# GpSimd's operations placed beside VectorE's clamps, V in three parts, a shorter head and another table, in a one-core mix of full and local attention

## The chip, the cores and the metric

The kernel runs on one core of a Trainium2 chip. The core has five engines that each work through their own list of instructions and wait for one another through semaphores: TensorE (PE in the profile; its weight loads are the row PEld), VectorE (DVE), ScalarE (ACT), GpSimd (POOL) and SyncE (SP), which here only issues DMA transfers. The metric is the time of one execution on the device in microseconds. Three timed runs of the kernel before gave 810.4, 808.63 and 810.71 us, a median of 810.4.

## What is computed

For one sequence of 2048 tokens with 640 features and 32 heads of 20 features, two attentions over the same x are mixed by a gate per token:

```python
x = A_x                                             # 1 x 2048 x 640, bf16
g = sigmoid((x * gate_w).sum(-1, keepdims=True))
a = A_ref(x, A_wqkv, A_wo)   # full softmax attention, every key for every query
b = B_ref(x, B_wqkv, B_wo)   # 8 keys per query: the token and 7 earlier ones, 2 apart
return g * a + (1 - g) * b
```

Branch A is most of the work: 32 heads x 2048 queries x 2048 keys of scores, exponentials and weighted sums.

## The kernel before

**Tiling of branch A.** Four heads form a quad q (8 quads), 512 queries a chunk qc (4 chunks). A pair (qc, q) is a group; there are 32, in the order of the list `GROUPS`: first the quads 0 to 3 of query chunks 0 and 1 in turn, then quads 4 to 7 of these chunks, then chunks 2 and 3. A group goes over 16 blocks of 128 keys and 4 heads, so it has 64 units, each a block of 128 keys x 512 queries of one head; 2048 units in all. `qk` (L1654) makes two or three units' scores in PSUM, `exp` (L1678) turns them into weights on ScalarE into `ebuf`, and `pv` (L1723) multiplies them by V (`vA`, with a column of ones that gives the sum) and adds into the bank `obank`, where a whole group is gathered.

**Units ridden on VectorE.** Some units don't go to ScalarE. They are taken in quads of up to four units (all heads of one key block, called d). VectorE clamps a unit's scores out of PSUM and rounds them to 16-bit integers whose bits are read as a bf16 weight (`uD`, L1668, called the clamp). To even out the error, three more copies of the whole quad, shifted by a constant, are made from `uD` (`eD`, L902, the shifted copies, in `gen_d`), and each is multiplied on PE by its own weighted copy of V. These weighted copies are `vS`: GpSimd multiplies the quad's V block by three constants (L894, also in `gen_d`, ahead of the shifted copies). `wanted` decides when a quad is opened and a unit ridden: two buffers of `uD` must allow it, and thresholds on VectorE's idle time and on how long the group still lasts.

**Closing a group.** `close` starts `gen_norm`: VectorE transposes `obank` to `oTt` (L863) and takes reciprocals of the sums (L867); GpSimd multiplies these by the gate (L869, 16 numbers per partition) and the 512 columns of `oTt` by the result (L875, called the norm product); VectorE transposes back (L877) and SP writes the pieces to `oTd` for the output projection. The last group does the products on VectorE.

**Side work.** Generators hand out small pieces of other work between the scores: `gen_v` projects V in two halves of 320 columns (quads 0 to 3, then 4 to 7), each over the 16 key blocks, with a cast by VectorE (L831); the first half starts with the loop, the second with group 1. `gen_kd` projects K in five chunks of features (VectorE L678 and L681, then DMAs into `kT`); chunk f may start at the group `KWAIT[f]`. `gen_qd` makes the scaled queries and their bounds, `gen_gate` the gate. `gen_bproj` and `gen_b` are branch B in eight units of 256 tokens (products on VectorE at L974 and L1073, sums on PE); they need V complete, because they reuse the memory of its weights. `gen_fold` projects both branches to the output.

**Order.** The order of every engine's list is written by a planner when the program is built. It goes through the 709 score tiles in turn, keeps an assumed time for each engine, and gives out side work as long as it fits before the next scores are due. Each task is given an assumed length and the buffers that it reads and writes; from these come the semaphore waits. Tasks marked `port`, and all of GpSimd's, are assumed not to run at the same time, since both engines then need the same way to SBUF. The table `PLAN` gives, from tile number on, 18 settings: slack before scores, when quads open, how far ahead VectorE may be booked, priorities.

**Head.** x comes in four blocks of 512 tokens. Nine warm-up matmuls run until the first block has landed; PE transposes each block (`turn`, L1369) into PSUM, ScalarE and VectorE copy it out (`x_out`), and PE projects K for quad 0 (L1392). After the first `turn` four more warm-up matmuls follow (L534). GpSimd pads the first K weights (L603) and fills `kT` for quads 1 to 7 with ones (L1441). `v_first` projects the first V block (320 columns).

Of the kernel before, what the change touches and what calls it, by code (L numbers as in the profile page):

```python
# [37 lines left out]
KWAIT = (0, 0, 3, 5, 7)  # L38
# [14 lines left out]
    0: ((0.3, 0.64), 0.31, 1.0, 2.5, 0.49, -0.95, -0.1, 11.8, 7.0, 6.03, 0.52, 0.85, 4.4, 4.0, 0.0, 0.64, 3, -1.5),  # L53
    5: ((0.29, 0.69), 0.16, 1.0, 6.6, 1.12, -1.6, 0.17, 11.8, 7.0, 7.54, 0.6, 0.62, 4.85, 4.42, 0.0, 0.65, 2, -3),
    10: ((0.29, 0.69), 0.01, 1.0, 6.6, 1.12, -1.6, 0.17, 11.8, 2.0, 7.54, 0.6, 0.62, 4.85, 4.42, 0.0, 0.65, 2, -3),
    15: ((0.3, 0.63), 0.39, 1.0, 5.5, 0.79, -1.37, -1.15, 7.47, 2.0, 6.29, 0.6, 0.62, 5.69, 3.17, -0.08, 0.63, 2, -3),
    30: ((0.34, 0.51), 0.25, 1.0, 5.5, 0.87, -1.26, -0.43, 13.15, 7.0, 4.65, 0.7, 0.51, 5.31, 4.81, 0.08, 0.39, 1, -3),
    35: ((0.34, 0.51), 0.25, 1.0, 5.5, 0.87, -1.6, -0.43, 9.86, 7.0, 4.65, 0.7, 0.43, 5.31, 3.66, 0.2, 0.61, 1, -3),
    40: ((0.34, 0.58), 0.25, 1.0, 5.5, 0.87, -1.6, -0.43, 8.24, 7.0, 4.65, 0.7, 0.43, 5.31, 3.66, 0.2, 0.61, 1, -3),
    45: ((0.34, 0.58), 0.25, 1.0, 5.5, 0.87, -1.6, -0.43, 8.24, 7.0, 5.73, 0.7, 0.43, 5.31, 3.66, 0.2, 0.61, 1, -3),  # L60
    65: ((0.34, 0.58), 0.25, 1.0, 5.5, 0.87, -1.6, -0.43, 8.24, 7.0, 5.73, 0.69, 0.43, 4.7, 4.27, 0.2, 0.61, 1, -3),
    80: ((0.34, 0.58), 0.25, 1.0, 5.5, 0.87, -1.6, -0.43, 8.24, 7.0, 5.73, 0.69, 0.36, 4.7, 4.27, 0.2, 0.61, 1, -3),
    85: ((0.2, 0.8), 0.39, 1.0, 1.0, 0.81, -0.84, -0.81, 6.61, 7.0, 8.75, 0.01, 0.61, 5.68, 4.3, 0.0, 0.71, 2, -3),
    100: ((0.2, 0.8), 0.39, 1.0, 1.0, 0.81, -0.84, -0.81, 4.77, 7.0, 8.75, 0.01, 0.61, 5.68, 4.3, 0.0, 0.71, 2, -3),
    105: ((0.2, 0.8), 0.39, 1.0, 1.0, 0.81, -0.84, -0.81, 4.77, 7.0, 8.75, 0.01, 0.61, 5.68, 3.61, 0.0, 0.86, 2, -6),
    115: ((0.2, 0.8), 0.39, 1.0, 1.0, 0.81, -0.84, -0.81, 4.77, 7.0, 8.75, 0.01, 0.61, 5.68, 3.61, 0.2, 0.86, 2, -6),
    120: ((0.2, 0.8), 0.39, 1.0, 1.0, 0.63, -0.84, -1.89, 4.77, 7.0, 8.75, 0.01, 0.61, 5.68, 3.61, 0.2, 0.86, 2, -6),
    125: ((0.2, 0.73), 0.39, 1.0, 1.0, 0.63, -0.84, -1.89, 4.77, 7.0, 8.75, 0.01, 0.61, 5.68, 3.61, 0.2, 0.86, 2, -6),
    130: ((0.22, 0.73), 0.39, 1.0, 1.0, 0.63, -0.84, -1.89, 4.77, 6.7, 8.75, 0.01, 0.61, 5.68, 3.61, 0.2, 0.86, 2, -6),
    135: ((0.22, 0.73), 0.39, 1.0, 1.0, 0.77, -0.84, -1.89, 4.77, 6.7, 8.75, 0.01, 0.61, 5.63, 3.61, 0.2, 0.86, 2, -6),  # L70
    145: ((0.19, 0.73), 0.39, 1.0, 1.0, 0.77, -0.84, -1.89, 4.77, 6.7, 8.75, 0.01, 0.61, 5.63, 3.61, 0.2, 0.98, 2, -6),
    150: ((0.34, 0.68), 0.01, 2.5, 1.0, 1.25, -1.06, 0.05, 7.4, 7.0, 10.69, 0.6, 0.55, 3.3, 5.42, 0.0, 0.61, 1, -1.5),
    155: ((0.26, 0.75), 0.39, 1.0, 1.0, 0.81, -1.29, -0.97, 6.5, 7.0, 7.16, 0.43, 0.75, 4.4, 4.0, 0.0, 0.71, 0, 0),
    160: ((0.31, 0.76), 0.33, 2.5, 1.0, 0.82, -1.6, -0.34, 11.8, 6.2, 6.64, 0.82, 0.44, 4.4, 4.12, 0.0, 0.55, 2, 0),
    165: ((0.31, 0.76), 0.33, 2.5, 1.0, 0.82, -1.6, -0.34, 10.41, 7.0, 6.64, 0.34, 0.44, 3.87, 4.12, 0.0, 0.66, 2, 0),
    170: ((0.31, 0.76), 0.33, 2.5, 1.0, 0.82, -1.17, -0.34, 10.41, 7.0, 6.64, 0.34, 0.44, 3.87, 4.12, 0.0, 0.7, 2, 0),
    175: ((0.3, 0.63), 0.07, 5.5, 6.3, 0.94, -1.06, 0.05, 7.4, 2.0, 8.96, 0.6, 0.67, 3.3, 5.42, -0.14, 0.53, 1, -1.5),
    180: ((0.3, 0.63), 0.07, 5.5, 6.3, 0.69, -1.06, 0.05, 7.95, 2.0, 8.96, 0.6, 0.67, 3.3, 5.42, -0.14, 0.53, 1, -1.5),
    185: ((0.3, 0.69), 0.19, 5.5, 6.3, 0.69, -1.06, 0.05, 7.95, 2.0, 8.96, 0.6, 0.6, 3.3, 5.42, -0.14, 0.53, 1, -1.5),
    205: ((0.3, 0.66), 0.25, 2.5, 1.0, 0.94, -1.6, 0.49, 9.86, 2.0, 5.3, 0.57, 0.43, 5.64, 3.66, 0.0, 0.61, 0, 0),  # L80
    210: ((0.29, 0.69), 0.16, 1.0, 2.5, 0.94, -1.37, 0.17, 9.99, 7.0, 7.54, 0.6, 0.62, 5.69, 5.04, 0.0, 0.54, 2, -3),
    215: ((0.31, 0.72), 0.39, 1.0, 1.0, 0.94, -1.6, -0.5, 9.86, 5.5, 6.93, 0.52, 0.73, 4.64, 4.42, 0.0, 0.67, 2, -3),
    225: ((0.23, 0.7), 0.25, 2.5, 2.5, 0.83, -1.37, 0.49, 7.4, 5.5, 6.11, 0.6, 0.67, 7.13, 5.42, 0.0, 0.61, 1, 0),
    230: ((0.3, 0.63), 0.25, 1.0, 2.5, 0.83, -1.37, 0.49, 7.4, 5.5, 6.11, 0.43, 0.67, 7.13, 5.42, -0.2, 0.61, 1, 0),
    235: ((0.3, 0.63), 0.25, 1.0, 2.5, 0.83, -1.37, 0.49, 7.4, 5.5, 6.11, 0.43, 0.67, 7.78, 5.42, 0.0, 0.61, 1, 0),
    240: ((0.29, 0.69), 0.16, 1.0, 1.0, 0.94, -1.37, 0.17, 9.99, 7.0, 7.54, 0.6, 0.62, 5.69, 5.04, 0.0, 0.54, 2, -3),
    245: ((0.29, 0.69), 0.07, 1.0, 6.3, 0.94, -1.06, 0.05, 9.99, 2.0, 7.54, 0.6, 0.67, 4.79, 5.04, 0.0, 0.54, 2, -3),
    250: ((0.29, 0.58), 0.39, 6.6, 2.5, 0.94, -1.26, -0.43, 7.15, 7.0, 6.93, 0.67, 0.73, 5.56, 4.42, 0.0, 0.67, 1, -3),
    260: ((0.3, 0.53), 0.39, 1.0, 2.5, 0.94, -1.26, -0.43, 7.4, 7.0, 8.84, 0.67, 0.73, 4.45, 4.42, 0.0, 0.67, 1, -3),
    265: ((0.3, 0.53), 0.39, 5.5, 2.5, 0.94, -1.26, -0.43, 7.4, 7.0, 8.84, 0.67, 0.69, 4.45, 4.42, 0.0, 0.67, 1, -3),  # L90
    270: ((0.29, 0.69), 0.07, 2.5, 2.5, 1.39, -1.2, 0.05, 5.48, 2.0, 8.84, 0.54, 0.55, 5.43, 4.07, 0.0, 0.69, 2, -3),
    280: ((0.29, 0.69), 0.07, 2.5, 2.5, 1.39, -1.2, 0.05, 5.48, 2.0, 8.84, 0.54, 0.54, 5.43, 4.07, 0.0, 0.46, 2, -3),
    290: ((0.29, 0.69), 0.07, 2.5, 2.5, 1.39, -1.49, 0.05, 9.99, 7.0, 8.84, 0.6, 0.54, 5.31, 5.04, 0.08, 0.46, 2, -3),
    295: ((0.29, 0.69), 0.24, 2.5, 1.0, 0.94, -0.86, -0.5, 7.4, 7.0, 7.54, 0.67, 0.45, 4.4, 4.81, 0.0, 0.77, 2, -3),
    305: ((0.23, 0.63), 0.25, 2.5, 2.5, 0.94, -1.29, 0.49, 7.4, 5.5, 6.11, 0.43, 0.43, 5.56, 3.83, 0.0, 0.61, 1, 0),
    315: ((0.3, 0.63), 0.16, 1.0, 2.5, 0.94, -1.46, 0.26, 6.5, 5.5, 7.16, 0.43, 0.75, 6.57, 4.3, -0.1, 0.43, 1, 0),
    320: ((0.3, 0.66), 0.25, 2.5, 2.5, 0.73, -1.17, 0.49, 7.4, 2.0, 5.3, 0.63, 0.52, 5.64, 3.24, 0.0, 0.61, 1, 0),
# [96 lines left out]
class _Sched:  # L194
# [7 lines left out]
    def __init__(self, nc, ctx):  # L202
# [10 lines left out]
        self.mode = None  # L213
        self.busy = []
        self.port = {"dve": [], "pool": []}
        self.dma_final = {}

    def ready(self, *keys, to="pe"):
        t = 0.0
# [1696 lines left out]
```

## Time and profile before

| | |
|---|---|
| timed runs | 810.4, 808.63, 810.71 us, median 810.4 |
| the profiled execution's own time | 809.44 us |
| its span, first to last instruction | 807.5 us |
| ScalarE busy | 779.4 us (97%) |
| TensorE busy | 751.3 us (93%) |
| VectorE busy | 721.5 us (89%) |
| GpSimd busy | 124.9 us (15%) |
| exponential tiles on ScalarE | 709, of 1024 or 1536 columns |
| clamps / shifted copies on VectorE | 380 / 285 |
| vS / norm products on GpSimd | 95 / 31 |

In a group of instructions the row has the line, the engine, the operation, output and input with their shapes, the count, then the busy time in us and the mean length of one in ns, then the idle time of the engine just ahead of them and what ended most of it. Neighbouring instructions of an engine overlap a little, so the busy time of a group is less than count times mean. In a row of a timeline stand start and length in us; in square brackets the idle time before it and what it waited for. In a row by stretch, each engine has its busy time and, in brackets, its instructions.

### The profile page before, as it was taken

The numbers are of one execution on the slowest core, as the hardware profiler recorded it, in microseconds if no ns is written. First come the engines' busy times: TensorE is split into PE (matmuls) and PEld (weight loads), VectorE is DVE, ScalarE is ACT, GpSimd is POOL, SyncE is SP. The second block draws the span as 40 slices with busy tenths as digits, with TensorE's granted clock in tenths as the row PEclk, the third lists the DMA queues.
The fourth block names the chain that finished last, engine by engine and source line by source line (L and its number), as shares of the span: only waits on it lengthen the run. The fifth ranks groups of instructions, "written<-read, shape, count | busy, mean of one in ns | idle before, by whom it ended". The sixth has DMA issues, their size and how long they took to land.

```text
span 807.5 us, 28461 instructions
## 1 busy us (share of the span) xinstructions
PE 751.3 (93%) x12073; PEld 284.8 (35%) x12073; DVE 721.5 (89%) x1243; ACT 779.4 (97%) x741; POOL 124.9 (15%) x196
## 2 busy tenths in 40 slices
PE   8999999999998898999999998999999899999987
PEld 5432322232333343233334333343333433334232
DVE  7686999999889999899988999998998899899892
ACT  4999999999999999999999999999999999999996
POOL 6010111111110221120111110101120111211110
PEclk9999999999999999999999999999999999999999
DMA  9111111011301131300013122013002210300121
GB/s 308 47 28 41 30 23 40 15 28 23 85 15 31 32 75 26 79 16 24 21 22 81 31 55 45 12 24 95 13 14 53 66 20 15 77 28 7 39 65 37
DMA packets 61154, 36.08 MB, mean 45 GB/s; under 512 B 26661, under 2 KB 59829, under 8 KB 61029
## 3 DMA queue, kind: packets, MB, share of 16 engines
q1 hardware_dynamic: 60740, 33.94, 17.2%
q8 instruction: 96, 1.57, 0.8%
q10 hardware_dynamic: 288, 0.33, 0.1%
q14 instruction: 30, 0.24, 0.1%
HBM read 12.85 MB, written 3.54 MB: 20 GB/s over the span
## 4 chain that ended last, share of the span: by engine, by line
DVE 29%; PE 27%; ACT 27%; issue 13%; SPq 1%; DMA 1%; POOL 0%; DVEq 0%; ACTq 0%
ACT ebuf L1678 27%; DVE uD L1668 11%; PE score L1654 8%; DVE eD L902 8%; PE obank L1723 7%; PE side L637 6%; DVE kvw L1073 3%; PE score L637 2%; DVE qkvB L948 2%; SPq L956 1%; DVE kvw L974 1%; DVE oB L1106 1%; PE score L1369 1%; DVE oTt L863 1%; PE obank L534 1%
## 5 line engine op out<-in xcount | busy, mean ns | idle before, releaser
L1678 ACT ACTIVATE ebuf<-score 128x1024 bf16<-128x1024 f32 (+1 forms) x709 | 767.7, 1225 | 11.7 <-PE score L1654 9.2
L1654 PE MATMUL score<-qT,kT 32*128 32x512 bf16 x1856 | 257.5, 384 | 30.6 <-ACT ebuf L1678 18.1
L1668 DVE TENSOR_SCALAR uD<-score 128x512 int16<-128x512 f32 x380 | 250.2, 678 | 19.3 <-PE score L1654 18.5
L902 DVE TENSOR_SCALAR eD<-uD 128x2048 int16<-128x2048 int16 x285 | 197.3, 717 | 2.6 <-PE obank L1723 1.5
L1723 PE MATMUL obank<-ebuf,vA 128*21 128x512 bf16 x1668 | 156.0, 385 | 4.4 <-DVE eD L902 1.6
L1654 PEld LDWEIGHTS score<-qT,kT 32*128 32x128 bf16 x1856 | 64.3, 91 | 231.4 <-ACT ebuf L1678 150.2
L894 POOL TENSOR_TENSOR vS<-vA,vw 128x252 bf16<-128x252 bf16 x95 | 68.2, 721 | 344.8 <-PE obank L1723 299.9
L1723 PE MATMUL obank<-eD,vS 128*21 128x512 bf16 x1140 | 99.3, 379 | 0.0
L637 PE MATMUL side<-xT,wBs 128*32 128x256 bf16 x2300 | 92.3, 281 | 2.0 <-DVE qkvB L948 1.6
L637 PEld LDWEIGHTS side<-xT,wBs 128*32 128x32 bf16 x2300 | 65.6, 142 | 30.2 <-issue 14.9
L1723 PEld LDWEIGHTS obank<-ebuf,vA 128*21 128x21 bf16 x1668 | 37.0, 89 | 88.2 <-issue 58.6
L869 POOL TENSOR_TENSOR rcp<-rcp,gA 128x16 f32<-128x16 f32 x31 | 7.2, 233 | 298.5 <-DVE rcp L867 289.6
L1073 DVE TENSOR_TENSOR kvw<-kvw,eB 128x2048 bf16<-128x2048 bf16 x40 | 49.0, 1242 | 1.3 <-DMA kvw<-qkvB 1.3
L974 DVE TENSOR_TENSOR kvw<-qkvB 128x2048 bf16<-128x2048 bf16 x40 | 49.0, 1243 | 0.0
L948 DVE CAST qkvB<-side 128x512 bf16<-128x512 f32 (+1 forms) x69 | 40.0, 590 | 0.9 <-PE side L637 0.5
L1723 PE MATMUL obank<-uD,vA 128*21 128x512 bf16 x380 | 37.1, 379 | 0.0
L1723 PEld LDWEIGHTS obank<-eD,vS 128*21 128x21 bf16 x1140 | 28.0, 92 | 18.1 <-issue 1.4
L875 POOL TENSOR_TENSOR oN<-oTt,rcp 128x512 bf16<-128x512 f32 x31 | 32.7, 1053 | 2.4
L863 DVE STREAM_TRANSPOSE oTt<-obank 128x512 f32<-128x512 f32 x32 | 22.6, 707 | 10.2 <-PE obank L1723 10.1
L637 PE MATMUL side<-xT,kvw 128*32 128x512 bf16 (+1 forms) x360 | 29.4, 382 | 1.4 <-DVE qkvB L678 1.3
L1654 PE MATMUL score<-woBp,kT 32*128 32x512 bf16 x192 | 27.9, 384 | 0.9 <-ACT ebuf L1678 0.6
L637 PE MATMUL side<-xT,WqP 128*32 128x512 bf16 x340 | 25.7, 382 | 0.1
(191 smaller groups left out, 548.8 us busy)
## 6 DMA issues: line engine op xcount, KB each, us to landing
kvw<-qkvB SPq DMA_DIRECT2D x128, 80.6 KB
wBs<-in_B_wqkv_dram SPq DMA_DIRECT2D x1, 2400.0 KB
WqP<-in_A_wqkv_dram SPq DMA_DIRECT2D x14, 160.0 KB
oTd<-oN SPq DMA_DIRECT2D x108, 20.0 KB
out_dram<-outsb SPq DMA_DIRECT2D x12, 160.0 KB
qT<-dst SPq DMA_DIRECT2D x93, 20.0 KB
kvw<-in_A_wqkv_dram SPq DMA_DIRECT2D x2, 800.0 KB
oTd<-in_A_x_dram SPq DMA_DIRECT2D x2, 640.0 KB
```

Source lines behind the costliest of these rows:

```text
L637: ins = e.matmul(o[j:k, :], l(j) if callable(l) else l[:, j:k], r, start=(first and i == 0), stop=(last and i == n - 1), skip_group_check= ...
L863: T("dve", 0.625, lambda e: e.transpose(oTt[:, :], obank[:, :]), reads=["obank"], writes=["oTt"])
L875: T(en, c2, lambda e: e.tensor_tensor(oo, ii, ib, ALU.mult), reads=["rcp", "oTt"], writes=["oN0"])
L894: T("pool", 0.607, lambda e: e.tensor_tensor(vS[:, d % 2, :, :], _ap(vA, (kb * NQ + q) * 4 * DV, [[0, K - 1], [1, 4 * DV]]), _ap(vw, 0, [[ ...
L902: T("dve", 0.065 + 0.1334 * n, lambda e, k=k, sl=sl: e.tensor_scalar(eD[:, sl % NS, 0:512 * n].bitcast(I16), uD[d % 2][:, 0:512 * n].bitca ...
L948: t = TB(dvc(n * TOK), lambda e, o=o, i=i: e.tensor_copy(o, i), reads=[("side", b)], writes=[key])
L974: TB(dvc(CH, 2), lambda e: e.tensor_tensor(o, i0, i1, ALU.mult), reads=["qB", "kB"], writes=[("prod", i)] + (["WkA", "WvA", ("WkP", 0)] if ...
L1073: TB(dvc(CH, 2), lambda e: e.tensor_tensor(o, i0, i1, ALU.mult), reads=["eB"] + [("vR", w4) for w4 in range(4)], writes=[("prod", i)], por ...
L1654: ins = e.matmul(o, kT[32 * j:32 * j + 32, q, kb * P:(kb + 1) * P], qT[qbuf[g]][32 * j:32 * j + 32, :], start=True, stop=True)
L1668: t = T("dve", 0.598, lambda e: e.tensor_scalar(uD[d % 2][:, 512 * i:512 * (i + 1)].bitcast(I16), side[x], UOFF, 0.0, op0=ALU.add, op1=ALU ...
L1678: exps[s] = T("act", actc(512 * n), lambda e: e.activation(ebuf[s % NE][:, 0:512 * n], score[s % 2][:, 0:512 * n], ACTF.Exp, scale=LN2 / S ...
L1723: ins = e.matmul(obank[32 * j:32 * j + DV, :], v, src, start=(kb == 0), stop=(last and k >= len(lst) - 4), skip_group_check=True)
```

## The change

There are five parts. First, the planner remembers the last VectorE task marked `port` (`last_port`), and a task can be told to wait for further tasks (`after`). Second, `vS` leaves `gen_d` for a generator of its own, `gen_vs`, added when a quad is opened; it, the small gate product and the norm product, which is now two halves of 256 columns, each wait in the planner for a "slot": right after a clamp has been written into VectorE's list the first waiting generator may go on, or after 4.0 us (vS) or 3.0 us (norm). The task then waits on the chip for the last `port` task of VectorE. The shifted copies wait in the planner until `vS` has been issued. Third, V is projected in three parts: quads 0 and 1, 2 and 3 (160 columns each), 4 to 7 (320 columns), started with the loop, with group 1 and with group 3. Fourth, in the head the four warm-up matmuls after the first transposes go, the fills of `kT` for quads 5 to 7 move into `gen_kd`, K's second chunk waits for group 2, and some assumed lengths are others. Fifth, `PLAN` has other rows (110 instead of 106).

```diff
-KWAIT = (0, 0, 3, 5, 7)
+KWAIT = (0, 2, 3, 5, 7)
 PLAN = {
-    0: ((0.3, 0.64), 0.31, 1.0, 2.5, 0.49, -0.95, -0.1, 11.8, 7.0, 6.03, 0.52, 0.85, 4.4, 4.0, 0.0, 0.64, 3, -1.5),
-    5: ((0.29, 0.69), 0.16, 1.0, 6.6, 1.12, -1.6, 0.17, 11.8, 7.0, 7.54, 0.6, 0.62, 4.85, 4.42, 0.0, 0.65, 2, -3),
...
+    0: ((0.3, 0.63), 0.16, 1.0, 1.0, 0.94, -1.37, -0.29, 4.03, 5.5, 8.32, 0.45, 0.75, 5.69, 5.04, -0.2, 0.54, 1, -3),
+    10: ((0.3, 0.63), 0.16, 1.0, 1.0, 0.94, -1.37, -0.29, 4.03, 6.2, 8.32, 0.45, 1.01, 5.69, 5.04, -0.2, 0.54, 1, -3),
...
+        for a in after:
+            add(a, True)
...
+        if port and stream == "dve":
+            self.last_port = t
...
+            for q in {1: (5,), 2: (6, 7)}.get(f, ()):
+                kt_fill(q)
...
-    def gen_v(half):
-        for kb in range(NV0 if half == 0 else 0, KBN):
+    VPART = ((0, 2), (2, 4), (4, NQ))
+    vpart = lambda q: 0 if q < 2 else 1 if q < 4 else 2
+
+    def gen_v(part):
+        q0, q1 = VPART[part]
+        c0, n = 4 * DH * q0, 4 * DH * (q1 - q0)
+        for kb in range(NV0 if part == 0 else 0, KBN):
...
+        if en == "pool":
+            yield ("slot", sch.avail["pe"] + SLOTW[1])
         T(en, c1, lambda e: e.tensor_tensor(rcp[:, :], rcp[:, :], gA[qc % 2][:, :], ALU.mult),
-          reads=["rcp", ("gA", qc % 2)], writes=["rcp"])
+          reads=["rcp", ("gA", qc % 2)], writes=["rcp"], after=last_port() if en == "pool" else ())
...
+        for i, n in ((0, 4),) if en == "dve" else ((0, 2), (2, 2)):
...
+            if en == "pool":
+                yield ("slot", sch.avail["pe"] + SLOTW[1])
+            T(en, c2 if n == 4 else 0.56, lambda e, oo=oo, ii=ii, ib=ib: e.tensor_tensor(oo, ii, ib, ALU.mult), reads=["rcp", "oTt"],
+              **{"accum" if i else "writes": ["oN0"]}, after=last_port() if en == "pool" else ())
...
-        while cur["pv"] < d - 1 or not done.get(("v", kb, q // 4)) or not done.get("vw"):
+        while not done.get(("vs", d)):
             yield ("cond",)
-        T("pool", 0.607, lambda e: e.tensor_tensor(
...
+    last_port = lambda: [sch.last_port] if sch.last_port else []
+
+    def gen_vs(d):
+
+        g, kb = dquads[d]
+        q = GROUPS[g][1]
+        while cur["pv"] < d - 1 or not done.get(("v", kb, vpart(q))) or not done.get("vw"):
+            yield ("cond",)
+        yield ("slot", sch.avail["pe"] + SLOTW[0])
+        if closed[d] and not ridden[d]:
+            return
+        T("pool", 0.607, lambda e: e.tensor_tensor(
+            vS[:, d % 2, :, :], _ap(vA, (kb * NQ + q) * 4 * DV, [[0, K - 1], [1, 4 * DV]]), _ap(vw, 0, [[1, K - 1], [0, 4 * DV]]), ALU.mult),
+          reads=[("vA", kb, vpart(q)), "vAones", "vw"], writes=[("vS", d % 2)], after=last_port())
+        done[("vs", d)] = True
...
+        elif req[0] == "slot":
+            if not force and now < req[1]:
+                return False
...
+    SLOTW = (4.0, 3.0)
+
+    def slot():
+
+        for ent in sorted(gens, key=lambda e: e[0]):
+            if ent[3][0] == "slot":
+                step(ent, 0.0, True)
+                return
...
     turn(0)
-    for i in range(4):
-        T("pe", 0.215, warm_up, reads=[("qabs", 0)], writes=["obank"])
     x_out(0)
...
+        if q < 5:
+            kt_fill(q)
...
+            add_gen(gen_vs(len(dquads) - 1), 1.0)
...
             bank_free[x] = t.end + LAT["dve"]
+            slot()
...
                 if g1 == 1:
                     add_gen(gen_gate(0), 1.5)
+                    add_gen(gen_v(1), 2.9)
+                if g1 == 2:
                     add_gen(gen_gate(1), 1.6)
-                    add_gen(gen_v(1), 3)
+                if g1 == 3:
+                    add_gen(gen_v(2), 3)
```

## The prediction

> **What bounds the kernel now.** I read the page's busy times first, then the groups of instructions by line, then the chain of the first 24 us, then VectorE's and GpSimd's timelines side by side, and last the busy times by stretch.
>
> The page and its costliest groups:
>
> ```profile
> PE 751.3 (93%) x12073; PEld 284.8 (35%) x12073; DVE 721.5 (89%) x1243; ACT 779.4 (97%) x741; POOL 124.9 (15%) x196
> ...
> L1678 ACT ACTIVATE ebuf<-score 128x1024 bf16<-128x1024 f32 (+1 forms) x709 | 767.7, 1225 | 11.7 <-PE score L1654 9.2
> ...
> L1668 DVE TENSOR_SCALAR uD<-score 128x512 int16<-128x512 f32 x380 | 250.2, 678 | 19.3 <-PE score L1654 18.5
> L902 DVE TENSOR_SCALAR eD<-uD 128x2048 int16<-128x2048 int16 x285 | 197.3, 717 | 2.6 <-PE obank L1723 1.5
> ```
>
> ScalarE's exponentials fill 767.7 of 807.5 us and wait 11.7 us. The first begins at 19.60 and the last ends at 799.5, so the span is a head of 19.6, a full ScalarE, and a tail of 8 us. Of the 2048 score units (one 128x512 block of one head), 1668 go to ScalarE and 380 are ridden on VectorE (a clamp, then three shifted copies per quad of four). The time can fall in two ways only: a shorter head or tail, or more units on VectorE.
>
> The head, from the chain that ended last, cut to its first 24 us (start, length, what):
>
> ```profile
> 5.24 1.88 PE score L1369 x20
> 7.12 0.86 PE obank L534 x4
> 7.99 1.12 PE score L1369 x20
> ```
>
> The four warm-up matmuls stand on the chain between the first and second transposed block of x.
>
> GpSimd against VectorE, two answers of the timeline, VectorE's lines first (start, length, what):
>
> ```profile
> 359.24 0.23 DVE L867 RECIPROCAL rcp<-oTt 128x16 f32<-128x16 f32 x1
> 359.40 0.62 DVE L1668 TENSOR_SCALAR uD<-score 128x512 int16<-128x512 f32 x1
> 359.94 1.51 DVE L902 TENSOR_SCALAR eD<-uD 128x2048 int16<-128x2048 int16 x1
> ```
>
> ```profile
> 359.55 0.22 POOL L869 TENSOR_TENSOR rcp<-rcp,gA 128x16 f32<-128x16 f32 x1 [7.85 <-DVE rcp L867]
> 359.85 1.06 POOL L875 TENSOR_TENSOR oN<-oTt,rcp 128x512 bf16<-128x512 f32 x1
> 360.85 1.06 POOL L894 TENSOR_TENSOR vS<-vA,vw 128x252 bf16<-128x252 bf16 x1
> ```
>
> A shifted copy (median 0.683 us) that meets the norm product takes 1.51, ending 0.55 after the product does; then vS (median 0.609) takes 1.06, behind the copy. The two never work at once. The clamp is different: the 78 clamps that overlap GpSimd take 0.673 on average, the others 0.680.
>
> The early stretches (columns: PE, PE's loads, VectorE, ScalarE, GpSimd busy):
>
> ```profile
> 30.00:40.00 10.00, 9.65 (x179) 3.93 (x171) 5.65 (x18) 9.95 (x10) 0.00 (x0) 1.00 0.10 20
> 50.00:60.00 10.00, 9.85 (x147) 3.06 (x139) 7.64 (x16) 10.00 (x10) 0.61 (x1) 1.00 0.25 54
> 70.00:80.00 10.00, 9.53 (x132) 2.86 (x132) 5.97 (x15) 10.00 (x10) 1.28 (x2) 1.00 0.28 56
> ```
>
> Early on PE is full and VectorE is not, and only 25 of the 380 clamps lie before 100 us.
>
> **The change, part by part.** The profiled execution took 809.44 us (span 807.5, 1.94 around it); the median of the three timed runs is 810.4, 0.1% above. The sum is made against 809.44.
>
> *Head.* Four warm-ups go: 0.86 us on the chain. The second block of x landed at 7.06 and its transposes began at 7.82, so they can begin near 7.17: 0.65 gained. Everything to the first exponential is PE's continuous chain (blocks three and four landed at 9.31 and 11.26, before 10.02 and 12.21, when they were used). Bounds: +0.86 at best; at worst the transposes fall back to the spacing of the first thirteen (0.107 instead of 0.055 us, twenty of them, 1.0 us), a loss of 0.2. I take 0.65, since the new gap is under 0.1 us. The three later kT fills (1.04 each) leave the head; the op they held (L1463, 1.26 us) gains nothing, being covered by the query projection that ends at 16.95. The halved first V block (0.84 us on PE, 0.49 on VectorE) is covered by the query scaling L1476, for which the first scores wait; without that cover it is worth 0.4. The order of SP's head DMAs does not change, only their assumed lengths.
>
> *GpSimd's slots.* Now 95 vS, 31 small gate products and 31 norm products become 95, 31 and 62. Each waits for the last VectorE op that uses both engines' way to SBUF and so starts beside the clamp behind it. What it removes: for L902 285 x (717-683) ns = 9.7 us; L974 and L1073 40 x (1243-1216) and 40 x (1242-1216) = 2.1; L770 18 x (356-288) = 1.2; smaller lines, summed from their overlaps, 1.8. Together 14.8 us of VectorE. What is left: GpSimd starts 0.08 after VectorE's op ends (359.47 to 359.55). The clamp starts 0.60 after that op's start and ends its turn at 1.20; vS, from 0.76, ends at 1.37, a half product (half of 1.053) at 1.29. After a clamp the next op is a copy or a B product in 129 of 380 cases. Where 0.17 to 0.19 us of GpSimd work remained, copies grew by 0.03 to 0.05. So 157 x 129/380 x 0.04 = 2.1 us stay. The 14 unslotted pad copies (L935) keep 0.6, and the three moved kT fills cost 0 to 2.7 (each can hold a copy for up to 0.9); I take 0.9.
>
> What hides the waits: a slotted op queues GpSimd's pad copies and the next vS behind it; a late vS delays the shifted copies (now begun only after vS is issued) and the slice matmuls. PE waited 0.3 us in all for vS, so 0 is taken; the rival of the slots, below, is this cover gone. The norm chain (after the first six groups 3 to 8 us from L863 to the end of L877) becomes up to 9 us longer. Its four or five oTd DMAs move behind SP's qT and B loads; oTt is next needed a group later, some 24 us: 0. Only the last GpSimd norm is near: closed at 776.1, its oN finished at 783.8, first needed at 796.1.
>
> The Trainium skill, "SBUF — State Buffer", section "Who interferes with whom", says that a VectorE op with at most one SBUF input outside the two-port modes leaves GpSimd alone; the clamps' 0.673 against 0.680 agree. It also says that whoever issues first holds the shared pair for its whole instruction while the other fully blocks, which taken strictly would leave 0.17 instead of 0.04 us per meeting; the first of the rivals below prices that.
>
> *V in three parts.* Casts of 320 columns start 0.40 us apart; at 1.05 ns a column (from 680 ns for 512 and 275 for 128) one of 160 takes 0.23. 31 x 0.23 + 16 x 0.40 against 31 x 0.40 is +1.2 us of VectorE. PE's columns stay the same.
>
> VectorE thus gains 14.8-2.1-0.6-0.9-1.2 = 10.0 us. A ridden unit costs 0.60 + 3 x 0.60/4 = 1.05 us there and spares ScalarE 0.45 (1.331/3 and 0.905/2 from start to start). With both full, a microsecond freed is worth 0.45/(1.05+0.45) = 0.30: 3.0 us, some 7 units. Bounds: 0 if it stays idle (VectorE idles 86 us already), 14.8 x 0.45/1.05 = 6.3.
>
> *Early stretch.* VectorE is idle for 19.5 of the 80 us from 20 to 100, against 6.4% from 100 to 700: 14.4 us too much. Half of the first V pass (15 x 0.35 us of PE) and the second K chunk (61.9 to 74.5, four matmul groups of 1.26, eight VectorE ops, seven kT DMAs at 76.5 to 81.1) move later; the table's first rows let rides open with 4.03 us of a group left instead of 11.8. Bounds: 0 to 14.4/1.05 x 0.45 = 6.2. I take a third of the idle time, 4 units, 1.8 us, since PE stays nearly full. The K chunk can slide: from 77 it ends near 90, two query steps of 8.2 us each (58.5 to 66.7) reach 106, and group 4 needs them at 122.6. Its DMAs pass four oTd and five qT issues on SP: 0, with 16 us of cover; beyond that ScalarE waits one for one.
>
> *The table* has no cost of its own; it decides how much of the two gains is taken.
>
> Sum: 809.44 - 0.65 - 3.0 - 1.8 = 804.0.
>
> **The rivals.**
> *The whole remainder is lost.* If a copy behind a clamp stands for all 0.17 us that vS still runs, 157 x 129/380 x 0.17 = 9.1 us stay instead of 2.1, VectorE gains 3.0 and the span 0.9: 806.1. For it: long meetings (359.94) end 0.55 after GpSimd whatever their start. Against: the short ones grew by 0.03 to 0.05.
> *No change in rides.* Freed VectorE time stays idle; only the head gains: 808.8. For it: 86 us of idle time. Against: from 100 to 700 it is only 6.4%.
> *Slots hold vS back (slower).* After each of 31 closes the norm's three steps stand ahead of vS, each for a clamp or a 3 us limit, and the quad's copies wait for vS. With w us of VectorE idle per close the loss is 31 x 0.30 x w; from w = 0.6 the whole gain is gone. Clamps come 1.97 us apart on average; at half of that, 1.0, it costs 9.3: 813.3. For it: vS at 360.85 directly behind the norm. Against: vS may now start with the first of a quad's four clamps.
> *B starts late (slower).* V's last part begins at group 3 (about 100) instead of group 1 (53); it ended at 212.6, and B's products start at 244.7. If it ends later, B slides with it. The last unit's output (L1106, 784.3) is 15 us before the last exponential; beyond that each us costs one, so 26 us late gives 804 + 11 = 815. Against: the eight units stand some 70 us apart and could close up.
> *More than forecast.* The early idle time is filled: 6.2 instead of 1.8, 799.6.
>
> **How the numbers follow.** Forecast 0.38 (its own range 801 to 807.9), the whole remainder 0.08, more 0.10, no change 0.14, slots 0.20, B late 0.10. A measurement here tells 0.3%, 2.4 us. Faster: 0.38+0.08+0.10+0.02 of the no-change case = 0.58; same: 0.12 of that case; slower: 0.30. The range 799.5 to 814 leaves out half of "more" (0.05), a third of the slots (0.07) and half of B late (0.05).
>
> **What would show it.** The first exponential near 18.95; L902's mean near 690 ns; 62 norm products near 0.53 us; some 391 clamps, about 35 of them before 100 us. It would be wrong if clamps do not grow, if VectorE's idle time after closes grows, or if vS becomes what PE waits for.

## The result and the profile after

The changed kernel takes 805.8 us (median of 7 runs, 801.13 to 807.74) where the kernel before, run beside it, takes 809.68 (7 runs): a ratio of 0.9949, 95% interval 0.9924 to 0.9974. It is faster by 0.5%, and 1.8 us above the forecast. The profiled execution is the quickest of the seven, 801.13 us with a span of 799.3; it must not be read as the median. Its own account shows where the gain came from, and the spread from 801 to 808 is a second question, taken up with the experiments.

The page of the kernel after, busy times and costliest groups:

```profile
PE 746.1 (93%) x12268; PEld 285.5 (36%) x12270; DVE 716.4 (90%) x1272; ACT 773.2 (97%) x745; POOL 123.8 (15%) x229
...
L1729 ACT ACTIVATE ebuf<-score 128x1024 bf16<-128x1024 f32 (+1 forms) x713 | 761.6, 1241 | 9.8 <-PE score L1704 8.9
...
L1718 DVE TENSOR_SCALAR uD<-score 128x512 int16<-128x512 f32 x387 | 256.1, 681 | 24.7 <-PE score L1704 23.2
L919 DVE TENSOR_SCALAR eD<-uD 128x2048 int16<-128x2048 int16 (+1 forms) x291 | 192.3, 683 | 3.5 <-PE obank L1774 2.5
...
L939 POOL TENSOR_TENSOR vS<-vA,vw 128x252 bf16<-128x252 bf16 x97 | 59.3, 612 | 404.9 <-DVE eD L919 186.9
L896 POOL TENSOR_TENSOR oN<-oTt,rcp 128x256 bf16<-128x256 f32 x62 | 39.1, 631 | 63.0 <-DVE eD L919 38.0
```

The shifted copies fell from 717 to 683 ns, the length that they have alone, and `vS` from 721 to 612. There are 387 clamps instead of 380. VectorE does more work in less time (716.4 us against 721.5).

GpSimd and VectorE around one close, two answers of the timeline (start, length, what):

```profile
359.01 0.62 POOL L896 TENSOR_TENSOR oN<-oTt,rcp 128x256 bf16<-128x256 f32 x1 [2.91 <-DVE kvw L1106]
359.57 0.25 POOL L968 COPY qkvB<-qkvB 128x80 bf16<-128x80 bf16 x1
359.78 0.62 POOL L896 TENSOR_TENSOR oN<-oTt,rcp 128x256 bf16<-128x256 f32 x1
361.03 0.61 POOL L939 TENSOR_TENSOR vS<-vA,vw 128x252 bf16<-128x252 bf16 x1 [0.63 <-DVE eD L919]
```

```profile
359.06 0.69 DVE L981 CAST qkvB<-side 128x512 bf16<-128x512 f32 x1
359.67 0.68 DVE L1718 TENSOR_SCALAR uD<-score 128x512 int16<-128x512 f32 x1
360.26 0.68 DVE L919 TENSOR_SCALAR eD<-uD 128x2048 int16<-128x2048 int16 x1
360.86 1.28 DVE L1718 TENSOR_SCALAR uD<-score 128x512 int16<-128x512 f32 x2
```

The first half product lies beside a cast and the second beside a clamp, both out of PSUM; `vS` begins only after the copy at 360.26, beside the next two clamps. The second half still runs when that copy begins, and the copy takes 0.68 all the same. Added up over all forms as in the prediction, what VectorE loses to overlaps fell from 14.8 to 1.1 us; 173 clamps now overlap GpSimd (78 before) and take 682 ns, as long as the others.

The chain of the first 24 us, cut to the transposes:

```profile
1.25 5.76 DMA oTd<-in_A_x_dram
7.02 0.05 issue
7.06 1.29 PE score L1414 x20
```

The second block is transposed as soon as it has landed; no warm-up stands ahead of it. The first exponential begins at 18.75 instead of 19.60.

The account of the two profiled executions, by the starts of the exponentials (0.904 us from start to start for a tile of 1024 columns and 1.331 for 1536; what is longer is called waiting):

| us | before | after | change |
|---|---|---|---|
| to the first exponential | 19.60 | 18.75 | -0.85 |
| tiles at full pace (1668 units in 709; 1661 in 713) | 747.7 | 744.9 | -2.8 |
| waiting between tiles | 32.0 | 26.9 | -5.1 |
| from the last exponential's end | 8.03 | 8.64 | +0.6 |

VectorE's and PE's busy time in the early and the middle stretch (columns: PE, its loads, VectorE, ScalarE, GpSimd, clock), first of the kernel before, then of the kernel after:

```profile
20.00:100.00 80.00, 77.74 (x1218) 27.20 (x1209) 60.54 (x129) 78.72 (x71) 6.48 (x10) 1.00 0.16 38
100.00:700.00 600.00, 560.82 (x9034) 210.49 (x9034) 561.61 (x944) 592.33 (x566) 93.47 (x143) 1.00 0.17 38
```

```profile
20.00:100.00 80.00, 75.76 (x1263) 26.02 (x1255) 68.30 (x146) 78.74 (x76) 11.80 (x19) 1.00 0.15 37
100.00:700.00 600.00, 563.52 (x9200) 214.15 (x9200) 550.61 (x953) 594.09 (x573) 87.87 (x167) 0.99 0.17 39
```

Early, VectorE's idle time fell from 19.5 to 11.7 us, and 37 clamps lie before 100 us instead of 25. From 100 us on it is the other way round: VectorE idles 49 instead of 38 us up to 700, and there are 350 clamps instead of 355 up to the end. The time freed in the middle did not go into rides. It shows as shorter waits, on the way from a clamp to the next scores, in the waits of PE, before and after (us in total, times, longest):

```profile
PE score L1654 <- DVE uD L1668: 8.2, 23, 0.7
```

```profile
PE score L1704 <- DVE uD L1718: 3.7, 10, 0.9
```

**The clock.** The last number but two of the row 100 to 700 after is 0.99. The granted clock is halved there for single stretches of 3.41 us, at 450.1, 484.2 and 641.2; before, there was none until the end. The first and the last of them with the stretch ahead, by busy times (same columns):

```profile
446.10:449.50 3.40, 1.82 (x21) 0.41 (x17) 2.95 (x4) 3.40 (x3) 0.00 (x0) 1.00 0.28 58
449.50:453.00 3.50, 3.41 (x47) 1.07 (x47) 2.95 (x8) 1.87 (x3) 0.22 (x1) 0.58 0.22 43
637.70:641.20 3.50, 2.00 (x34) 0.73 (x34) 3.34 (x4) 3.43 (x3) 0.00 (x0) 1.00 0.20 60
641.20:644.60 3.40, 3.40 (x42) 0.99 (x38) 3.36 (x6) 1.46 (x2) 0.61 (x1) 0.50 0.02 5
```

PE was hardly more than half busy, and the stretch after that ran at 0.50 (0.58 where the cut is not exact), with ScalarE down to 1.87 and 1.46 us of work. The gap at 446, by the timelines of VectorE, of PE and of ScalarE:

```profile
446.55 2.36 DVE L1106 TENSOR_TENSOR kvw<-kvw,eB 128x2048 bf16<-128x2048 bf16 x2 [0.91 <-DMA kvw<-qkvB]
```

```profile
448.51 0.39 PE L1704 MATMUL score<-qT,kT 32*128 32x512 bf16 x3 [0.95 <-ACT ebuf L1729]
449.59 0.40 PE L1774 MATMUL obank<-ebuf,vA 128*21 128x512 bf16 x4 [0.70 <-DVE oTt L879]
```

```profile
452.77 1.45 ACT L1729 ACTIVATE ebuf<-score 128x1536 bf16<-128x1536 f32 x1 [1.63 <-PE score L1704]
```

PE had nothing to do at two points: it waited 0.95 us for ScalarE, and 0.70 us for the transposition of a closed group, which stood on VectorE behind two products of branch B that had themselves waited 0.91 us for their load. In the half-clock stretch ScalarE then waited 1.63 us for scores.

The three stretches begin 10 and 46 times 3.41 us apart: they lie on a fixed grid, so whether a gap in PE's work fills one of its cells differs from run to run. Counted on all positions of that grid from PE's records (less 0.165 us for the modelled end of each matmul), 1.6 cells lie under half occupied in the trace before and 3.7 after; the three cells ahead of the halved ones were 0.36, 0.49 and 0.41 occupied. The kernel fills such gaps itself with fillers, four matmuls whose result nobody uses, with weights of zero or into a score buffer that is free (L1795, L1744 before): 119 before, 84 after. The Trainium skill, "TensorE: Matmul & The Clock Gate", section "What's actually happening", describes a gate that is throttled by default and judges free-running windows of about 3.4 us, dropping to half rate after an idle one; the grid of 3.41 us and the 0.50 agree, but here a window was not idle, only about half filled.

### The profile page after: what moved, and what is told of

Read it like the earlier page. It is cut to its first block, busy times and chain, and to the rows that moved or that the text cites. A ratio compares the mean times of both kernels' runs of the same rounds, so it can differ in the third digit from the quotient of the medians.

```text
span 799.3 us, 29024 instructions
## 1 busy us (share of the span) xinstructions
PE 746.1 (93%) x12268; PEld 285.5 (36%) x12270; DVE 716.4 (90%) x1272; ACT 773.2 (97%) x745; POOL 123.8 (15%) x229
## 4 chain that ended last, share of the span: by engine, by line
PE 39%; ACT 28%; DVE 15%; issue 13%; SPq 2%; DMA 1%; POOL 0%; ACTq 0%; DVEq 0%
ACT ebuf L1729 27%; PE score L1704 11%; PE obank L1774 10%; PE side L646 10%; DVE uD L1718 6%; DVE eD L919 3%; PE score L646 3%; SPq L989 2%; DVE kvw L1106 2%; DMA kvw<-qkvB 1%; PE obank L1795 1%; DVE qkvB L981 1%; PE side L1116 1%; DMA oTd<-in_A_x_dram 1%; DVE oTt L879 1%
## 5 line engine op out<-in xcount | busy, mean ns | idle before, releaser
L1718 DVE TENSOR_SCALAR uD<-score 128x512 int16<-128x512 f32 x387 | 256.1, 681 | 24.7 <-PE score L1704 23.2
L919 DVE TENSOR_SCALAR eD<-uD 128x2048 int16<-128x2048 int16 (+1 forms) x291 | 192.3, 683 | 3.5 <-PE obank L1774 2.5
L939 POOL TENSOR_TENSOR vS<-vA,vw 128x252 bf16<-128x252 bf16 x97 | 59.3, 612 | 404.9 <-DVE eD L919 186.9
L1774 PE MATMUL obank<-eD,vS 128*21 128x512 bf16 x1161 | 103.0, 380 | 0.0
L896 POOL TENSOR_TENSOR oN<-oTt,rcp 128x256 bf16<-128x256 f32 x62 | 39.1, 631 | 63.0 <-DVE eD L919 38.0
L1007 DVE TENSOR_TENSOR kvw<-qkvB 128x2048 bf16<-128x2048 bf16 x40 | 47.6, 1217 | 0.0
L1704 PE MATMUL score<-woBp,kT 32*128 32x512 bf16 x192 | 29.5, 384 | 2.4 <-ACT ebuf L1729 1.7
L646 PE MATMUL side<-kvw,xT 128*32 128x160 bf16 (+1 forms) x760 | 28.0, 262 | 2.2 <-DVE vA L847 1.7
```

The source lines that it names most:

```text
L646: ins = e.matmul(o[j:k, :], l(j) if callable(l) else l[:, j:k], r, start=(first and i == 0), stop=(last and i == n - 1), skip_group_check= ...
L896: T(en, c2 if n == 4 else 0.56, lambda e, oo=oo, ii=ii, ib=ib: e.tensor_tensor(oo, ii, ib, ALU.mult), reads=["rcp", "oTt"], **{"accum" if ...
L919: T("dve", 0.065 + 0.1334 * n, lambda e, k=k, sl=sl: e.tensor_scalar(eD[:, sl % NS, 0:512 * n].bitcast(I16), uD[d % 2][:, 0:512 * n].bitca ...
L939: T("pool", 0.607, lambda e: e.tensor_tensor(vS[:, d % 2, :, :], _ap(vA, (kb * NQ + q) * 4 * DV, [[0, K - 1], [1, 4 * DV]]), _ap(vw, 0, [[ ...
L1007: TB(dvc(CH, 2), lambda e: e.tensor_tensor(o, i0, i1, ALU.mult), reads=["qB", "kB"], writes=[("prod", i)] + (["WkA", "WvA", ("WkP", 0)] if ...
L1704: ins = e.matmul(o, kT[32 * j:32 * j + 32, q, kb * P:(kb + 1) * P], qT[qbuf[g]][32 * j:32 * j + 32, :], start=True, stop=True)
```

## The experiments

The kernel before was run beside each; its medians were 809.71 to 810.02 us, its clock 0.998. The planner reacts to any change of its input, so most experiments keep the order of every engine's list as planned and change only what is written out from it.

**The changed kernel once more** (after_again), for its spread.

> The changed kernel as it is, for a comparison on one chip. Theory of the clock: its times spread over some 6 us, because 3 to 6 windows of 3.41 us at half clock fall into each execution (mean granted clock 0.986 to 0.993); 805 us in the median. Rival (the spread comes from DMA arrival alone): the times don't go with the clock.

Measured: 805.07 us (12 runs, 801.73 to 810.14), ratio 0.995 (0.993 to 0.997). The spread is the kernel's own, and with the seven runs above it goes with the clock: correlation -0.77 over 19 runs, 1.3 us for each halved stretch that the mean clock (0.986 to 0.998) stands for.

**The slots without their wait** (after_no_wait): the lists are those of the changed kernel, but GpSimd's operations no longer wait on the chip for VectorE's last port task. They begin as soon as their data are there.

```diff
-        for a in after:
-            add(a, True)
...
+        for d in after:
+            start = max(start, d.end + lat(d, stream))
```

> The changed kernel with the same order on every engine, but without the wait of vS and the norm products for VectorE's last port operation: GpSimd begins each as soon as its data are there. Theory that the wait on the chip does the work: shifted copies and B products meet GpSimd again, the mean of a shifted copy goes from 683 back to 705 to 720 ns, VectorE loses 8 to 14 us, and the time rises by 2 to 5 us. Rival, that the planned order alone is enough: the copies stay under 690 ns and the time within 1 us of the changed kernel.

Measured: 816.04 us (6 runs, 813.74 to 819.64), ratio 1.0084 (1.0058 to 1.011). Its page:

```profile
L1730 ACT ACTIVATE ebuf<-score 128x1024 bf16<-128x1024 f32 (+1 forms) x713 | 766.7, 1208 | 19.2 <-PE score L1705 16.3
...
L920 DVE TENSOR_SCALAR eD<-uD 128x2048 int16<-128x2048 int16 (+1 forms) x291 | 204.6, 725 | 2.4 <-PE obank L1775 1.4
...
L940 POOL TENSOR_TENSOR vS<-vA,vw 128x252 bf16<-128x252 bf16 x97 | 75.8, 782 | 431.1 <-PE obank L1775 386.9
```

The copies are slow again (725), 89 of them overlap GpSimd instead of 19, and VectorE loses 20.4 us instead of 1.1. The time rises by 11 us, more than twice what was expected: 0.57 us for each microsecond of stall, if all of it is the stall's. ScalarE's idle time ahead of its tiles is 19.2 instead of 9.8, but 4.0 of it is one wait that ends at 24.1 us, behind a pause of PE like the one shown below with after_fill43; by the 41st exponential this execution is 3.8 us behind the changed kernel's. Whether the other five runs had that pause is not known; if all had it, the price is 0.37. That PE waits for a clamp 9.2 us in all, instead of 3.7, fits the stall.

**The kernel before with slots** (before_slots): its plan and its 380 clamps, but the norm products in halves, and 119 of the 188 operations (95 `vS`, 31 gate products, 62 halves) wait for VectorE's last port task ahead of a clamp.

```diff
+                        if start >= at - 0.1 and c.idx not in taken and v is not None and not needs(v, p) and not needs(c, p):
+                            taken.add(c.idx)
...
+                            if not any(d.dom == "cmp" and d.stream == "dve" for d in q.deps):
+                                q.deps = q.deps + [v]
```

> The kernel before with its plan and its 380 clamps unchanged, but the norm product issued in halves, and 119 of GpSimd's 188 operations (vS, gate product, half products) made to wait for VectorE's last port operation ahead of its next clamp. Theory that the stalls of VectorE lie largely on the path even without a new table (0.54 us for each us of stall, as the changed kernel without its waits showed): the mean of a shifted copy falls from 717 to 690 ns, some 10 us of stall go, and the time falls by 4 to 6 us. Rival, that the freed time is only worth something if the table then opens more rides: the stalls go, the time stays within 1.5 us of the kernel before, or rises because vS comes late.

Measured: 806.69 us (11 runs, 803.96 to 809.83), ratio 0.9962 (0.9947 to 0.9976). Its copies:

```profile
L976 DVE TENSOR_SCALAR eD<-uD 128x2048 int16<-128x2048 int16 x285 | 190.0, 691 | 2.6 <-PE obank L1797 1.5
```

The stall fell from 14.8 to 3.3 us, and the time by 3.0, less than the 4 to 6 expected, with not one ride more: 0.27 us for each microsecond. PE's waits for a clamp fell from 8.2 to 2.1 us. So the stalls lie partly on the path. The gain needs no exchange of units, which the prediction took for the only way. The clock (0.992 to 1.0) did not fall with the slots.

**The four warm-ups put back** (after_warm) into the changed kernel, behind the transposes of the first block, nothing else moved.

```diff
-        T("pe", 1.13 if tcc else 1.9, fn, reads=[("xs", tcc), "ident"], writes=tkeys(s_))
+        def with_warm(e):
+            ins = fn(e)
+            for i in range(4):
+                warm_up(e)
+            return ins
+
+        T("pe", 1.13 if tcc else 1.9, fn if tcc else with_warm, reads=[("xs", tcc), "ident"], writes=tkeys(s_))
```

> The changed kernel with the four warm-up matmuls issued again behind the first transposes, the plan unchanged. Theory: the first exponential moves from 18.75 back to 19.5, and the time rises by 0.7 to 0.9 us. Rival (the kT fills and the smaller first V block made the head shorter): the first exponential stays under 19.0.

Measured: 806.36 us (8 runs, 800.74 to 807.86), ratio 0.9953 (0.9934 to 0.9972), 0.6 to 1.3 above the changed kernel's medians, within their spread, so the time alone decides nothing. The first exponential begins at 19.62, 0.87 later. The chain of its head, and that of before_slots, which has the same warm-ups:

```profile
1.22 4.02 PE obank L543 x9
5.24 2.09 PE score L1414 x20
7.33 0.86 PE obank L543 x4
8.19 1.12 PE score L1414 x20
```

```profile
0.73 4.30 DMA oTd<-in_A_x_dram
5.04 0.05 issue
5.08 1.29 PE score L1443 x20
6.37 0.86 PE obank L601 x4
7.24 1.12 PE score L1443 x20
```

The first block's twenty transposes took 2.09 us in one execution and 1.29 in the other. Where they are slow, the warm-ups push the second block from 7.06 to 8.19; where they are fast, to 7.24 only, and the first exponential of before_slots begins at 18.70 with its warm-ups in place. The head's gain is 0.87 in executions of the first kind and about 0.2 or less in the others.

**The new code with the old table** (new_code_old_table), against the changed kernel only the rows of `PLAN` differ; the first of each:

```diff
 PLAN = {
-    0: ((0.3, 0.63), 0.16, 1.0, 1.0, 0.94, -1.37, -0.29, 4.03, 5.5, 8.32, 0.45, 0.75, 5.69, 5.04, -0.2, 0.54, 1, -3),
...
+    0: ((0.3, 0.64), 0.31, 1.0, 2.5, 0.49, -0.95, -0.1, 11.8, 7.0, 6.03, 0.52, 0.85, 4.4, 4.0, 0.0, 0.64, 3, -1.5),
```

> The changed code with the table of the kernel before, so the planner orders everything anew. Its lists hold 343 clamps instead of 387. Theory that a table only fits the code that it was made for: 44 units more on ScalarE at 0.45 us are 20 us, and the time is 825 to 850. Rival (the code change alone brings the gain and the table little): 803 to 810.

Measured: 853.79 us (2 runs, clock 0.989 and 0.983), ratio 1.0548 (1.053 to 1.0566), 4 us above the range expected. Clamps fall to 343, ScalarE gets 1705 units (763.8 us at full pace), and it waits 60 us. A table belongs to the code that it was made with, so the parts of this change can't be had one at a time through the planner. That is why V in three parts was not tried by itself.

**More fillers** (after_filled and before_filled). In each kernel the list of PE is as planned, with more fillers written in where the trace shows PE under-occupied, 167 in the one and 170 in the other. They add zeros to `obank`.

```diff
+                        if sname == "pe":
+                            for _ in range(MORE.get(i, 0)):
+                                self.more(eng)
...
+    def more(e):
+        for j in range(4):
+            e.matmul(obank[32 * j:32 * j + 32, :], zero[:, :], xT[:, 0, 0:512], start=False, stop=False, skip_group_check=True)
```

> The changed kernel with the same plan on every engine, and 167 more filler matmuls on TensorE (each four 32-column strips, zeros added to the open obank), put where its trace shows TensorE idle for 0.2 us or more inside a 3.4 us stretch that is under 62% occupied. Theory of the clock: windows at half clock go from about 4 to under 1, the mean clock rises to 0.996 or more, and with 1.0 to 1.8 us for each window the median falls by 3 to 6 us, to 800 to 802. Rival: the clock windows cost nothing because ScalarE is the bound; then it stays at 805 or becomes slower by up to 167 x 0.22 us that collide with other work.

> The kernel before, its plan unchanged, with 170 more filler matmuls put by the same rule into its own trace's gaps. Theory of the clock: its trace leaves 1.6 windows under half occupancy on average over all positions of the window grid, so it gains only 1 to 3 us (807 to 809). Rival: no change or slower.

Measured: after_filled 803.96 us (6 runs, 802.37 to 807.21), ratio 0.9937 (0.9912 to 0.9961), clock 0.997 to 1.0; before_filled 813.81 (6 runs, 813.32 to 814.44), ratio 1.005 (1.0032 to 1.0069), clock 0.999 to 1.0. Both expectations of the time missed. Fillers aren't free: the kernel before had hardly any clock to regain and lost 4.1 us, 24 ns for each filler. By that price 167 of them cost 4.0 us in the changed kernel, whose median fell by 1.1 to 1.8, a change within the spread of its runs; so the clock would have given back 5 to 6. That was an inference, and the next kernel puts it to the test.

**Fillers where they count** (after_fill43): 43 fillers, only in the gaps that bring a stretch of 3.41 us under its mark, the plan unchanged. It was run twice, since the first profile fell on the one run with a lowered clock.

```diff
+MORE = {101: 1, 583: 2, 604: 1, 606: 1, 677: 1, 680: 2, 744: 1, 869: 2, 1042: 2, 1074: 1, 1079: 2, 1088: 1, 1089: 2, 1163: 1, 1495: 1, 1499: 2, 1513: 1, 1560: 4, 1583: 2, 1625: 2, 1809: 1, 1990: 5, 2218: 1, 2395: 2, 2410: 1, 2416: 1}
```

> The changed kernel with its plan unchanged and only 43 more filler matmuls, each in a gap that two traces of it show at least 0.25 us long, and only as many as lift every 3.4 us stretch to 55% occupancy where the open obank allows it. Over 19 executions of the changed kernel the time went down by 1.3 us for each 3.41 us window at half clock less (0.0021 of mean clock). Theory that the windows cost this and that most of the 167 fillers of the run before collided with other work: mean clock 0.995 or more and a median of 801 to 803. Rival, that slow executions have both late work and low clock from one cause (late DMAs), and the windows themselves cost nothing: the clock rises and the median stays at 804.5 to 806.

> The kernel of after_fill43 once more, since the profiled execution there was its one execution with a lowered clock: a second profile, to see where an execution at full clock has its exponentials waiting. Windows under 50%: under 1.5. Waiting between exponentials 22 to 24 us instead of 26.9 in the changed kernel's profile, clock 0.999 or 1.0, median 798 to 801.

Measured: 799.59 us (5 runs), ratio 0.987 (0.9855 to 0.9884), better than the 801 to 803 expected, and 800.81 (4 runs), ratio 0.9893 (0.9853 to 0.9934). Seven of the nine runs have a clock of 0.999 or 1.0 and take 797.98 to 801.85 us; the two at 0.995 take 805.1 and 805.9. This version beats both kernels. The exponentials of the second profile, a run at full clock:

```profile
L1733 ACT ACTIVATE ebuf<-score 128x1024 bf16<-128x1024 f32 (+1 forms) x713 | 761.7, 1241 | 8.6 <-PE score L1708 7.5
```

They wait 25.2 us in all by the account above (26.9 in the changed kernel's profile, 22 to 24 expected), and the rest of that account is as it was, so this execution's 799.77 us is 9.67 under the profile of before: 0.67 by the head, 2.8 by units, 6.8 by waiting, less 0.6 in the tail.

One of those two is the first profile. PE stood still in it at 20.9 us, and one of its two mid-run stretches at half clock, at 24.1, followed (PE's timeline):

```profile
20.45 0.45 PE L650 MATMUL score<-kvw,xT 128*32 128x160 bf16 x16
23.46 0.25 PE L650 MATMUL score<-kvw,xT 128*32 128x160 bf16 x4 [2.57 <-issue]
```

It stopped inside a run of twenty like matmuls, and waited for no other engine that the profile shows. By the 41st exponential this execution is 4.2 us behind the second profile. The profiles of after_no_wait and new_code_old_table have the same pause in the same run of matmuls (2.55 and 2.64 us), and the half-clock stretch with it. The DMA records point to a cause: a packet of 16 KB of the queue q8, whose kind is "instruction", starts at 20.93, 20.67 and 20.81 us in these three, within 0.1 us of the end of PE's last matmul, and takes 1.0 to 1.1 us; in the six other profiles of the changed kernel and its variants it starts between 15.1 and 17.9, and PE doesn't stop. So PE may have waited for instructions that came late. This is not shown: no run moved that packet, PE begins again only 1.4 to 1.5 us after it has landed, and in before_filled and before_slots, where PE's list is another, it starts at 20.65 and 20.81 without a pause.

**Fewer fillers** (after_no_fill and before_no_fill): every filler cut from four matmuls of 32x512 to one of 32x64, the plans unchanged.

```diff
-            for j in range(4):
-                ins = e.matmul(o[32 * j:32 * j + 32, :], w[:, 32 * j:32 * j + 32] if best else w[:, :], xT[:, 0, 0:512], start=bool(best),
+            ins = e.matmul(o[0:32, 0:64], w[:, 0:32] if best else w[:, :], xT[:, 0, 0:64], start=bool(best),
```

> The changed kernel with the same lists on every engine, but each of its 84 fillers (four zero matmuls of 32x512, 0.216 us) cut to one zero matmul of 32x64, so that PE is idle where it was filled. By the trace of the changed kernel the mean number of 3.41 us windows in which PE is under 50% occupied grows from 3.7 to 9.6. If such windows cost the clock and the time (1.34 us each, from the 19 executions of the changed kernel): granted clock about 0.98, +8 us for six more windows, less 2 us for fillers that stood in the way (24 ns each, from before_filled): about 811. Rival, fillers are only work in the way and the clock follows something else: clock as the changed kernel's (0.986 to 0.998), 803 to 805.

> The kernel before with the same lists, its 119 fillers cut in the same way. Windows under 50% grow from 1.6 to 7.5 by its trace. If such windows cost: granted clock 0.98 to 0.985 instead of 0.998, +9 us (1.59 us each), less 3 us for the fillers gone: about 816. Rival: clock stays at 0.998, 806 to 809.

Measured: after_no_fill 807.99 us (10 runs, 803.1 to 813.12), ratio 0.997 (0.9944 to 0.9995), clock 0.979 to 0.991; before_no_fill 814.26 (8 runs, 812.15 to 816.19), ratio 1.0046 (1.0029 to 1.0064), clock 0.987 to 0.995. With less work on PE both clocks fell, as the clock theory said. The kernel before became slower by 4.2 us, clear of its spread; the changed kernel by 2.2 to 2.9 us, just at the edge of its own. The sizes were overestimated (811 and 816 expected). Two stretches of after_no_fill that follow on one another:

```profile
647.50:650.90 3.40, 0.42 (x4) 0.09 (x1) 2.67 (x3) 2.10 (x2) 0.00 (x0) 1.00 0.13 37
650.90:654.30 3.40, 3.06 (x31) 0.95 (x31) 3.40 (x6) 1.02 (x1) 0.61 (x1) 0.51 0.00 0
```

With this, one plan has been run with three amounts of filler, 38 runs in all (after, after_again, after_fill43 twice, after_no_fill). By the mean granted clock of a run:

| clock | runs | median us |
|---|---|---|
| under 0.984 | 6 | 809.3 |
| 0.984 to 0.988 | 6 | 807.0 |
| 0.988 to 0.992 | 13 | 805.1 |
| 0.992 to 0.9965 | 5 | 803.6 |
| above | 8 | 799.7 |

The correlation is -0.88 and the line through them falls by 1.1 us for each halved stretch of 3.41 us. What makes a gap also makes a wait (the pause at 20.9 us does both), so the correlation alone would prove little; that the time falls when only such unused matmuls are added, 43 of them, and rises when they are made smaller, is what shows the cause.

## Why the prediction came out right

The time was met, but not by the terms of its sum, and so in part by luck: without the loss of clock the change is worth some 10 us (799.7 against 809.8, the median of the runs of before beside these), not 5.4, and the clock took 5 to 6 of them back. Two errors of about that size, waits that the sum had at nothing and a clock that it did not have at all, cancelled.

*Head.* 0.65 was expected and 18.95; the profile has 18.75. The mechanism is right: the second block is transposed when it lands. Not seen was that the first block's transposes take 1.29 us in some executions, where next to nothing is gained. The lower bound of the prediction, the slow pace moving to the second block, did not come: it took 1.29 us.

*GpSimd's slots, the stall.* Right, and better than taken: 1.1 us left instead of 3.6, copies at 683 instead of 690. The remainder behind a clamp cost less than the 2.1 us worked out, so the first rival (0.17 us for each meeting) falls: the copies that met 0.17 to 0.19 us of GpSimd's work grew by 0.03 to 0.06, as the sum had it, and there were fewer meetings, 19 copies in all. after_no_wait shows that the wait does it. The half product was mis-sized: 0.63 us instead of 0.53, since 0.18 us of it doesn't shrink (estimated from 1.053 for 512 columns and a median of 0.619 for 256).

*The exchange rate.* This step failed as a mechanism. It said that freed time on VectorE is worth something only through rides, 0.30 us each, some 7 units. From 100 us on, rides fell by 5 and VectorE idles more, as in the rival of no change; yet the time fell, because stalled copies had held up the next scores: PE's waits for a clamp go with the stall at a fixed plan, from 8.2 to 2.1 us where it is taken out (before_slots) and from 3.7 to 9.2 where it is put back (after_no_wait). There a microsecond of stall is worth 0.27 us, and 0.37 to 0.57. In the account, units gave 2.8 us where the sum had 3.0 and 1.8 together, and waiting, which it had at nothing, gave 5 to 7, of which the slots' own share isn't separated from that of the table.

*Early stretch.* Right in kind, too small in size: 12 clamps more before 100 us (4 were given to this step, 10 expected there from both gains), and 7.8 us less idle time. Units in all: 7 fewer on ScalarE instead of 11, worth 2.8 us instead of 4.8.

*Tail.* The sum left it as it was; it grew by 0.6 us. After the last exponential PE still has 28 matmuls of side work (1.51 us) and 64 of the last output on the chain, where before the last norm's steps stood there.

*The table.* "No cost of its own" was the worst sentence. The new plan comes with 84 fillers instead of 119; PE falls under half occupancy more often, and the clock with it. It costs the 5 us above, and 43 fillers bring it back. Whether it is the table or the order of the new code that thins out PE isn't separated: the slots alone left the clock as it was (before_slots), but the new code with the old table ran at 0.983 and 0.989, with some 204 fillers in its trace.

*V in three parts* was not isolated. Its last cast comes at 183.4 instead of 212.6, not later.

*The rivals.* Slots hold `vS` back: no. PE's waits for `vS`, 0.3 us before, are gone after, and copies wait for nothing new. VectorE's idle time after a close, a sign named in the prediction, did not grow: on average 0.91 us of the 12 us after it, against 1.01. The norm chain did become longer, 5 to 14 us against 3 to 8 after the first six groups, about as forecast. B late: no. Its first product (L1007) begins at 261.0 instead of 244.7, its last at 737.8 instead of 739.6; the units closed up. But VectorE's waits for B's loads grew from 1.3 to 3.1 us; one of these (0.91) stands ahead of the gap of PE at 446, another (1.33) ahead of that at 638. More than forecast: by the number without the loss of clock it was this, for another reason than the one given.

## What to carry to other kernels

When an engine's stalls are removed, ask what waits for its results before converting the time into work: here, after the first 100 us, the freed time stayed idle and the gain came from shorter waits. When a new order thins out an engine's work, look at that engine's occupancy in the grid of the clock and not only at its share of the span: 93% busy on average held stretches under half. And fillers are a dose, not a setting: 43 in the right gaps gained 5 us, 167 gained 1 to 2 at most, and 170 where the clock was nearly full cost 4.

## What the runs showed of the hardware beyond this

- The granted clock of TensorE was halved for whole stretches of 3.41 us on a fixed grid after a stretch in which it was less than about half occupied. Over the 13 profiles, from 18 us on, counted as above on each profile's own grid, all 20 full-clock cells up to 0.413 occupied were followed by a halved one, 7 of 37 between 0.42 and 0.50, and none above. So half is no sharp mark. On one plan, runs at a mean clock of 0.9965 and above take 799.7 us, runs under 0.984 809.3.
- A filler of 0.216 us cost 24 ns of the whole time (4.1 us for 170) in the kernel before, where it was written into gaps of PE in stretches under 62% occupied but had hardly any clock to regain.
- Twenty transposes at the head took 1.29, 1.88 or 2.09 us in different executions of the same instructions, with the granted clock shown as 1.00. The same page of the Trainium skill, section "What's actually happening", says that the number of slow matmuls at the start varies from run to run with the phase of the window; the varying times agree with that, though the rows of the clock don't show it.
- A shifted copy that began while GpSimd's `vS` or norm product still ran grew by what was left of that operation, less 0.13 to 0.14 us. In the traces before and after this holds for 37 of the 38 such copies with 0.15 us or more left: they grew by 0.03 to 0.06 us with 0.17 to 0.19 left, by 0.14 with 0.28, by 0.41 with 0.55. In the one exception `vS` began only 0.007 us ahead of the copy and took the delay itself (1.16 us).
